# Half of one gated product per block handed from VectorE to ScalarE and GpSimd, in two of three blocks

## The chip, the cores and the metric

The kernel runs on one core of one Trainium2 chip. A core has five engines that work side by side, each through its own queue and in order: TensorE (matmuls, from SBUF into PSUM), VectorE, ScalarE, GpSimd, and SyncE, which here only issues DMAs. Engines wait for one another by semaphores. The metric is the device time of one execution in microseconds, the median of several runs. In the profile the engines are called PE, DVE, ACT, POOL and SP; PEld is TensorE's weight load.

## What is computed

An attention block with 32 inducing points over four batches of 12416 tokens, followed by a gated feed-forward layer of width 1536 over all 49664 tokens:

```python
def mab(q, kv):
    s = scale * (q @ kv.transpose(0, 2, 1))
    s = s - s.max(-1, keepdims=True)
    a = np.exp(s)
    a /= a.sum(-1, keepdims=True) + 1e-09
    return a @ kv
h = mab(I, x)                 # (B, 32, 128)
x = mab(x, h)                 # (B, 12416, 128), then seen as (49664, 128)

gate = 1.0 / (1.0 + np.exp(-(x @ w_gate)))
val = x @ w_val
return (gate * val) @ w_out
```

## The kernel before

The second attention's result is never formed. Its normalised weights `a2` (32 per token) are kept, and the products `h @ w_gate` and `h @ w_val` are folded into one small matrix `hw` per batch, so that gate and value of a token come from matmuls over 32 rows. The sigmoid is written as a tanh: gate times value is half of (tanh(g/2) + 1) times v, and the half is applied at the end.

*Blocks and steps.* 512 tokens (four chunks of 128) are a block; the 1536 features are twelve slices of 128, numbered j. A block is eight steps that alternate between two slices (wide, 1024 columns, two PSUM banks) and one slice (narrow, 512 columns, one bank): steps 0, 2, 4, 6 are wide, 1, 3, 5, 7 narrow. There are 96 such blocks, and four small ones of 128 tokens, one at the end of each batch: 776 steps in all, numbered t in the list `steps`.

*One step.* `gate(t)` (L545) issues the gate matmuls into `g_ps` (L535) and a tanh on ScalarE that writes `t` (L551). `product(t)` (L555) issues the value matmuls into `v_ps` (L535 too) and one VectorE instruction (L560) that adds 1 to `t`, multiplies by `v_ps` and writes `u`. PSUM has eight banks, all given out once: two for wide gates (`g2`), two for wide values (`v2`), one each for narrow gates (`g1`) and values (`v1`), one for side work (`m`), one for the accumulated result (`acc`). So a value matmul of a wide step waits until the product of the wide step before it has read `v_ps`, and a gate matmul until the tanh two steps earlier has read `g_ps`.

*The order.* It is written out by hand in the main loop (L690): for step t the product of t, then the gate of t+2, then in even steps a slot of side work (`beside`, L666), in odd steps projections (`project`, L580). `room` counts the projections that a call may issue, two units for each; before, it is 6 or 8, that is three or four. The queue of projections goes in order of j; each multiplies a slice of `u` by `wo16` into `acc` (L590). After a block's twelfth projection, ScalarE scales `acc` by one half into `o16` (L597, `o` in the profile), SyncE issues a DMA that transposes it into `on` (L599), and twelve steps later GpSimd issues the store to DRAM (L608). The next block's first projection waits until `o` has read `acc`.

*Side work.* `stage2` makes `a2` for the coming blocks: scores (L346), their maximum `nmx` on VectorE (L357), `hi` and `lo` on GpSimd (L361, L363), an Exp `e` on ScalarE (L379), the sums on GpSimd (L387), a reciprocal `rs` on VectorE (L405), `a2n` on GpSimd (L407), a transposing DMA into `a2r`. `stage1` does the first attention for the next batch: scores with their maximum `nm` (L169), an Exp `a1T` (L181), a transposing DMA, sums copied to `hst` by ScalarE (L217); `combine` joins the groups of a batch, with `hx` on GpSimd (L279, L290), and ends in `hw` (`hwt`, L336). Each is a generator that `beside` advances by one piece per slot; one holder at a time has the bank `m`. `stage2` is started 20 slots ahead of its use (`S2_LEAD`).

*Buffers.* `u` has six buffers of each width, `t` four.

Of the kernel before, what the change touches and what calls it, by code (L numbers as in the profile page):

```python
# [16 lines left out]
P = 128  # L17
# [3 lines left out]
S1_LAG = 6  # L21
S2_LEAD = 20


@with_exitstack
def kernel(
# [30 lines left out]
    s2p = ctx.enter_context(tc.tile_pool(name="s2p", bufs=2))  # L57
    up = ctx.enter_context(tc.tile_pool(name="up", bufs=6))
    tp = ctx.enter_context(tc.tile_pool(name="tp", bufs=4))
    op = ctx.enter_context(tc.tile_pool(name="op", bufs=8))  # L60


# [86 lines left out]

    summed = [0] * B  # L150

    def s1_dims(s):
# [3 lines left out]

    def s1_score(b, s, tag):
        c0, n = groups[s]
        ng, w, R = s1_dims(s)
        s1 = ps.tile([P, 512], F32, tag=tag, name="s1_ps")  # L160
        for g in range(ng):
            nc.tensor.matmul(  # L162
                s1[32 * g : 32 * g + 32, 0 : w * P],
                indT[:],
                xT[b][:, c0 + g * w : c0 + (g + 1) * w, :].rearrange("c j t -> c (j t)"),
                start=True,
                stop=True,
            )
        nc.vector.tensor_reduce(  # L169
            out=nm1s[b % 2][0:R, s : s + 1],  # L170
            in_=s1[0:R, 0 : w * P],
            axis=AX.X,
            op=ALU.max,
            negate=True,
        )
        return s1
# [12 lines left out]

    def s1_turn_pe(b, s, a1T):  # L190
        ng, w, R = s1_dims(s)
        aT = ps.tile([P, 4, P], F16, tag="m", name="aT_ps")
# [10 lines left out]

    def s1_sum(b, s, a1, tag):
        c0, n = groups[s]
        ng, w, R = s1_dims(s)
# [136 lines left out]

    def s2_score(b, c, j0, j1, s2):
        for j in range(j0, j1):
            nc.tensor.matmul(  # L346
# [20 lines left out]

    def s2_exp(n, s2, hi, lo):
        for t_, last in ((hi, False), (lo, True)):
            nc.tensor.matmul(  # L370
# [129 lines left out]
    for b in range(B):  # L500
        for s, (c0, n) in enumerate(groups):
            first_step[(b, s)] = len(steps)
            for k in range(0, n, BC):
# [5 lines left out]
                while j < NJ:  # L509
                    cnt = min(2 * per, NJ - j)  # L510
                    if nb == BC and idx % 2 == 1:
                        cnt = 1
                    steps.append(dict(b=b, c=c0 + k, nb=nb, j0=j, cnt=cnt))
                    j += cnt
# [40 lines left out]
    def product(t):  # L555
        st = steps[t]
        hidden_mm(st, "v")
        k, w = st["ext"]
        st["u"] = up.tile([P, k, 512], F16, tag=f"u{k}", name="u16")
        nc.vector.scalar_tensor_tensor(  # L560
            out=st["u"][:, :, 0:w],
            in0=st["t"][:, :, 0:w],
            scalar=1.0,
            in1=st["v"][:, :, 0:w],
            op0=ALU.add,
            op1=ALU.mult,
        )

    accs = {}
# [3 lines left out]
    for key in dict.fromkeys((st["b"], st["c"]) for st in steps):  # L573
        mine = [t for t in range(NST) if (steps[t]["b"], steps[t]["c"]) == key]
        of = {j: t for t in mine for j in range(steps[t]["j0"], steps[t]["j0"] + steps[t]["cnt"])}
        row = sorted(of)
        queue += [(of[j], j, j == row[0], j == row[-1]) for j in row]
    queue.reverse()

    def project(upto, now, room):  # L580
        while queue and queue[-1][0] < upto and room > 0:
# [4 lines left out]
            if first:  # L586
                accs[key] = ps.tile([P, 512], F32, tag="acc", name="acc_ps")
            acc = accs[key]
            k, col = place(st, j)
            nc.tensor.matmul(  # L590
                acc[:, 0:W], wo16[:, j, :], st["u"][:, k, col : col + W], start=first, stop=last
            )
            room -= 2 if st["nb"] == BC else 1
# [71 lines left out]

    def beside(slot):  # L666
        slot_now[0] = slot
# [6 lines left out]
        while work and work[0][0] <= slot:  # L674
            _, first, make = work.pop(0)
            active.append(dict(it=make(), ask=False, first=first))
        for gen in sorted(active, key=lambda e: e["first"]):
            advance(gen)
# [11 lines left out]
    for t in range(NST):  # L690
        product(t)
        gate(t + 2)
        if t % 2 == 0:
            beside(t // 2)
        else:
            project(t - 1, t, 6 if waiting(t - 1) <= 3 else 8)
        flush_stores(t)
# [32 lines left out]
```

## Time and profile before

| | us |
|---|---|
| median of three runs | 794.26 |
| lowest and highest | 793.11, 795.95 |
| the profiled execution | 795.01 |
| its span, first to last instruction | 793.1 |
| VectorE busy in the span | 745.4 |
| ScalarE busy | 672.8 |
| TensorE busy | 670.7 |
| GpSimd busy | 238.2 |
| products (L560), 388 wide and 388 narrow, mean | 1.219 and 0.676 |
| tanh (L551), 388 wide and 388 narrow, mean | 1.029 and 0.605 |
| `o` (L597), 96 of full width, mean | 0.605 |
| granted TensorE clock, mean | 0.967 |

A group of the profile shows a line, an engine and an operation, what it writes and reads, the count, then the busy time in us, the mean of one in ns, and the idle time of the engine just before these instructions with what ended it. The busy time of an engine is the union of its instructions' times; on VectorE and ScalarE an instruction's record reaches into the next one's by 0.1 us or so, so that starts lie closer together than durations say. In the timeline a line gives the start, the length, the engine and the group; neighbours of one kind are merged and counted (x3).

### The profile page before, as it was taken

What the parts mean: (1) busy time and instruction counts of PE and PEld (TensorE: products, weight loads), DVE (VectorE), ACT (ScalarE), POOL (GpSimd) and SP (SyncE); (2) the same over time, 40 slices, a digit from 0 to 9 for tenths busy, and PEclk for the clock granted to TensorE, in tenths of its full rate; (3) what the DMA queues carried; (4) which work ended last, traced back from release to release, by engine and by line L of the source; (5) the groups of instructions that cost most, each with busy time, mean ns of one, the idle gap of its engine ahead of it and who ended that gap; (6) DMA issues with size and microseconds to landing.
All of it is one profiled execution on the core that took longest, in us unless ns stands there. A gap on an engine that the chain in (4) does not pass through costs nothing.

```text
span 793.1 us, 13966 instructions
## 1 busy us (share of the span) xinstructions
PE 670.7 (85%) x4729; PEld 230.8 (29%) x4729; DVE 745.4 (94%) x948; ACT 672.8 (85%) x1001; POOL 238.2 (30%) x396
## 2 busy tenths in 40 slices
PE   6588889888888888888888888988888888888884
PEld 4222223222232222322222222322323222223221
DVE  4689999999999999999998999999999999999994
ACT  4389989888989999878988898988898898899993
POOL 4131341532331422444404123143233133133200
PEclk9679999999999999989999999999999999999997
DMA  9958654536439566355338754241431431441421
GB/s 178 204 108 168 120 111 84 103 77 116 87 75 198 95 102 138 81 98 100 64 80 163 131 93 91 57 81 47 83 86 43 90 87 28 100 87 40 103 60 46
DMA packets 171015, 77.44 MB, mean 98 GB/s; under 512 B 154784, under 2 KB 155328, under 8 KB 170944
## 3 DMA queue, kind: packets, MB, share of 16 engines
q1 hardware_dynamic: 150672, 37.23, 28.8%
q0 software_dynamic: 20272, 39.33, 21.0%
q8 instruction: 37, 0.61, 0.3%
q14 instruction: 34, 0.28, 0.1%
HBM read 27.80 MB, written 25.43 MB: 67 GB/s over the span
## 4 chain that ended last, share of the span: by engine, by line
DVE 42%; PE 24%; issue 21%; ACT 10%; DMA 2%; POOL 0%; POOLq 0%; ACTq 0%; DVEq 0%
DVE u L560 37%; PE acc_ps L590 11%; PE v_ps L535 9%; ACT t L551 8%; DMA xn<-in_x_dram 2%; DVE nmx L357 2%; PE s_ps L370 1%; DVE nm L169 1%; PE g_ps L535 1%; ACT a1T L181 1%; ACT o L597 1%; DVE rs L405 1%; DVE hwt L336 0%; PE hp_ps L210 0%; PE s_ps L346 0%
## 5 line engine op out<-in xcount | busy, mean ns | idle before, releaser
L560 DVE SCALAR_TENSOR_TENSOR u<-t,v_ps 128x1024 f16<-128x1024 f16 (+1 forms) x776 | 693.1, 947 | 19.0 <-PE g_ps L535 7.3
L551 ACT ACTIVATE t<-g_ps 128x1024 f16<-128x1024 f32 (+1 forms) x776 | 598.8, 817 | 81.5 <-PE g_ps L535 67.0
L535 PE MATMUL v_ps<-a2r,hwt 32*128 32x512 f16 (+1 forms) x1188 | 294.7, 374 | 94.8 <-DVE u L560 87.6
L590 PE MATMUL acc_ps<-u,wo 128*128 128x512 f16 (+1 forms) x1200 | 325.2, 383 | 1.4 <-ACT o L597 0.7
L535 PE MATMUL g_ps<-a2r,hwt 32*128 32x512 f16 (+1 forms) x1188 | 297.4, 381 | 0.8 <-ACT t L551 0.6
L535 PEld LDWEIGHTS <-hwt 32*128 32x128 f16 x2400 | 102.8, 91 | 355.0 <-issue 346.7
L590 PEld LDWEIGHTS <-wo 128*128 128x128 f16 x1200 | 86.1, 98 | 145.3 <-issue 99.3
L407 POOL TENSOR_TENSOR a2n<-e,rs 128x2048 f16<-128x2048 f16 (+2 forms) x28 | 87.3, 3119 | 82.2 <-DVE rs L405 73.7
L608 POOL DMA_DIRECT2D out_dram<-on x100 | 57.0, 570 | 143.8 <-DMA on<-o 134.1
L597 ACT ACTIVATE o<-acc_ps 128x512 f16<-128x512 f32 (+1 forms) x100 | 59.2, 592 | 9.5 <-PE acc_ps L590 7.1
L361 POOL CAST hi<-nmx 128x16 bf16<-128x16 f32 (+3 forms) x29 | 5.7, 195 | 203.1 <-DVE nmx L357 203.0
L387 POOL TENSOR_TENSOR sum<-e 128x256 f32<-128x256 f16 (+1 forms) x27 | 16.0, 591 | 70.2 <-ACT e L379 70.2
L387 POOL TENSOR_TENSOR sum<-sum 128x128 f32<-128x128 f32 (+3 forms) x108 | 31.3, 290 | 8.5
L76 POOL DMA_DIRECT2D xn<-in_x_dram x28 | 15.4, 557 | 11.1 <-DMA xn<-in_x_dram 7.2
L346 PE MATMUL s_ps<-hT,xT 128*128 128x32 f16 x388 | 18.2, 180 | 0.6
L181 ACT ACTIVATE a1T<-s_ps,nm 128x512 f16<-128x512 f32 (+1 forms) x28 | 17.9, 639 | 0.4 <-DVE nm L169 0.4
L169 DVE TENSOR_REDUCE nm<-s_ps 128x1 f32<-128x512 f32 (+1 forms) x28 | 17.3, 618 | 0.5 <-PE s_ps L162 0.5
L346 PEld LDWEIGHTS <-xT 128*128 128x128 f16 x388 | 13.5, 97 | 13.4 <-issue 13.1
L357 DVE TENSOR_REDUCE nmx<-s_ps 128x16 f32<-128x512 f32 (+3 forms) x29 | 17.3, 596 | 0.0
L379 ACT ACTIVATE e<-s_ps 128x512 f16<-128x512 f32 (+3 forms) x29 | 15.2, 524 | 1.5 <-PE s_ps L370 1.5
L454 ACT COPY xT<-xt_ps 128x1024 f16<-128x1024 f16 x6 | 6.1, 1012 | 10.8 <-DVE xT L453 10.8
L453 DVE COPY xT<-xt_ps 128x1024 f16<-128x1024 f16 x6 | 4.1, 692 | 9.6 <-PE xt_ps L451 9.6
(78 smaller groups left out, 182.1 us busy)
## 6 DMA issues: line engine op xcount, KB each, us to landing
out_dram<-on POOLq DMA_DIRECT2D x96, 256.0 KB, 2.6
xn<-in_x_dram POOLq DMA_DIRECT2D x24, 512.0 KB, 8.5
on<-o SPq DMA_TRANSPOSE x100, 2.4
a2r<-a2n SPq DMA_TRANSPOSE x28, 6.0
wg<-in_moe_w_gate_dram POOLq DMA_DIRECT2D x1, 384.0 KB, 16.4
wv<-in_moe_w_val_dram POOLq DMA_DIRECT2D x1, 384.0 KB, 16.5
wo<-in_moe_w_out_dram POOLq DMA_DIRECT2D x1, 384.0 KB, 16.2
xT<-xn SPq DMA_TRANSPOSE x21, 4.7
```

Source lines behind the costliest of these rows:

```text
L169: nc.vector.tensor_reduce(out=nm1s[b % 2][0:R, s : s + 1], in_=s1[0:R, 0 : w * P], axis=AX.X, op=ALU.max, negate=True,)
L181: nc.scalar.activation(out=a1T[0:R, 0 : w * P], in_=s1[0:R, 0 : w * P], func=AF.Exp, bias=nm1s[b % 2][0:R, s : s + 1], accum_out=l1s[b % 2 ...
L346: nc.tensor.matmul(s2[:, j, :], xT[b][:, c + j, :], hT16[b][:], start=(j == 0), stop=False, skip_group_check=True,)
L357: nc.vector.tensor_reduce(out=nmx[:, 0:n], in_=s2[:, 0:n, :], axis=AX.X, op=ALU.max, negate=True)
L387: nc.gpsimd.tensor_tensor(out=d[:, 0:n, :], in0=src[:, :, 0:w], in1=src[:, :, w : 2 * w], op=ALU.add)
L407: eng.tensor_tensor(out=a2n[:, 0:n, :, :], in0=e[:, 0:n, :].unsqueeze(2).to_broadcast((P, n, 4, m)), in1=rs[:, 0:n].unsqueeze(2).unsqueeze ...
L535: nc.tensor.matmul(pt[:, k, col : col + W], hw[st["b"]][r : r + 32, j // 2, :], a2r[r : r + 32, o : o + nb, :].rearrange("p j t -> p (j t) ...
L551: nc.scalar.activation(out=st["t"][:, :, 0:w], in_=st["g"][:, :, 0:w], func=AF.Tanh, scale=0.5)
L560: nc.vector.scalar_tensor_tensor(out=st["u"][:, :, 0:w], in0=st["t"][:, :, 0:w], scalar=1.0, in1=st["v"][:, :, 0:w], op0=ALU.add, op1=ALU. ...
L590: nc.tensor.matmul(acc[:, 0:W], wo16[:, j, :], st["u"][:, k, col : col + W], start=first, stop=last)
L597: nc.scalar.mul(out=o16[:, 0:W], in_=acc[:, 0:W], mul=0.5)
L608: nc.gpsimd.dma_start(ov[st["b"], :, c : c + nb, :], on[:, 0:nb, :])
```

## The change

`SHARE(block)` picks two of every three blocks, 64 in all. In these the wide product of step 0 is split: VectorE computes the first of its two slices (512 columns, `near`). For the second, ScalarE copies the value from PSUM to SBUF (`vc`, f32), GpSimd adds 1 to the second half of `t` (`t1`, f32) and multiplies the two (`far`, f16). The projection that reads `far` (j = 1) is put last in its block. `u` gets five buffers instead of six, `t` three instead of four.

The order changes in three places. The slot of side work two steps ahead of a split product is skipped (loads and new generators still enter, none is advanced). In other even steps where the side work has issued nothing that counts in `filled` (scores, transposes, sums and the correction matmuls of the Exp), one projection may be issued, if more than two are waiting and the next isn't the first of a block. In odd steps `room` is 2 (one projection) behind a split product, else 6 with up to four waiting (before: up to three) and 8 with more.

```diff
+def SHARE(block):
+    return block % 3 != 2
...
-    up = ctx.enter_context(tc.tile_pool(name="up", bufs=6))
-    tp = ctx.enter_context(tc.tile_pool(name="tp", bufs=4))
+    up = ctx.enter_context(tc.tile_pool(name="up", bufs=5))
+    tp = ctx.enter_context(tc.tile_pool(name="tp", bufs=3))
...
+    vp = ctx.enter_context(tc.tile_pool(name="vp", bufs=2))
...
-                    steps.append(dict(b=b, c=c0 + k, nb=nb, j0=j, cnt=cnt))
+                    steps.append(
+                        dict(b=b, c=c0 + k, nb=nb, j0=j, cnt=cnt, off=nb == BC and idx == 0 and SHARE(blocks))
+                    )
...
-        nc.vector.scalar_tensor_tensor(
-            out=st["u"][:, :, 0:w],
-            in0=st["t"][:, :, 0:w],
+        mine = 1 if st["off"] else k
+        near = nc.vector.scalar_tensor_tensor(
+            out=st["u"][:, 0:mine, 0:w],
+            in0=st["t"][:, 0:mine, 0:w],
             scalar=1.0,
-            in1=st["v"][:, :, 0:w],
+            in1=st["v"][:, 0:mine, 0:w],
             op0=ALU.add,
             op1=ALU.mult,
         )
+        if st["off"]:
+            vc = vp.tile([P, 512], F32, tag="vc")
+            far = nc.scalar.copy(out=vc[:], in_=st["v"][:, 1, :])
+            tc.declare_no_dep(far.ins, near.ins, reason="each reads a bank of its own")
+            t1 = vp.tile([P, 512], F32, tag="t1", bufs=1)
+            nc.gpsimd.tensor_scalar_add(out=t1[:], in0=st["t"][:, 1, :], scalar1=1.0)
+            st["far"] = vp.tile([P, 512], F16, tag="far", name="far", bufs=3)
+            nc.gpsimd.tensor_tensor(out=st["far"][:], in0=t1[:], in1=vc[:], op=ALU.mult)
...
-        row = sorted(of)
+        late = 1 if steps[mine[0]]["off"] else NJ
+        row = sorted(of, key=lambda j: (j == late, j))
...
-            nc.tensor.matmul(
-                acc[:, 0:W], wo16[:, j, :], st["u"][:, k, col : col + W], start=first, stop=last
-            )
+            u = st["far"][:] if st["off"] and k == 1 else st["u"][:, k, col : col + W]
+            nc.tensor.matmul(acc[:, 0:W], wo16[:, j, :], u, start=first, stop=last)
...
-    def beside(slot):
+    def beside(slot, rest):
...
+        if rest:
+            return
         for gen in sorted(active, key=lambda e: e["first"]):
             advance(gen)
...
         if t % 2 == 0:
-            beside(t // 2)
+            was = filled[0]
+            beside(t // 2, t + 2 < NST and steps[t + 2]["off"])
+            if filled[0] == was and waiting(t - 1) > 2 and not queue[-1][2]:
+                project(t - 1, t, 2)
         else:
-            project(t - 1, t, 6 if waiting(t - 1) <= 3 else 8)
+            room = 2 if steps[t - 1]["off"] else 6 if waiting(t - 1) <= 4 else 8
+            project(t - 1, t, room)
```

More of the change, by code (lines that the diff above doesn't have):

```diff
@@ L150 @@
     summed = [0] * B
+    filled = [0]
     def s1_dims(s):
@@ L157, in s1_score @@
     def s1_score(b, s, tag):
+        filled[0] += 1
         c0, n = groups[s]
@@ L190, in s1_turn_pe @@
     def s1_turn_pe(b, s, a1T):
+        filled[0] += 1
         ng, w, R = s1_dims(s)
@@ L204, in s1_sum @@
     def s1_sum(b, s, a1, tag):
+        filled[0] += 1
         c0, n = groups[s]
@@ L344, in s2_score @@
     def s2_score(b, c, j0, j1, s2):
+        filled[0] += 1
         for j in range(j0, j1):
@@ L368, in s2_exp @@
     def s2_exp(n, s2, hi, lo):
+        filled[0] += 1
         for t_, last in ((hi, False), (lo, True)):
```

## The prediction

> **What bounds the kernel now.** I read the page's busy shares first, then its slices, then the groups by shape, and last the timeline of a quiet stretch around 400 us. The page's part 1, and the rows of part 2 for the two engines that the change loads and unloads:
>
> ```profile
> PE 670.7 (85%) x4729; PEld 230.8 (29%) x4729; DVE 745.4 (94%) x948; ACT 672.8 (85%) x1001; POOL 238.2 (30%) x396
> ...
> DVE  4689999999999999999998999999999999999994
> ACT  4389989888989999878988898988898898899993
> ```
>
> VectorE is at nine tenths or more nearly everywhere between the start and the tail; ScalarE has about a tenth to give. The groups by shape (busy us, then mean ns of one):
>
> ```profile
> L560 DVE SCALAR_TENSOR_TENSOR u<-t,v_ps 128x1024 f16<-128x1024 f16 x388 | 472.8, 1219 | 16.9 <-PE g_ps L535 6.9 <-ACT t L551 4.4 <-ACT o L597 1.8
> ...
> L597 ACT ACTIVATE o<-acc_ps 128x512 f16<-128x512 f32 x96 | 58.1, 605 | 8.0 <-PE acc_ps L590 5.6
> ...
> L279 POOL TENSOR_TENSOR hx<-hst,w 128x896 f32<-128x896 f32 x3 | 5.0, 1677 | 23.4 <-ACT w L273 23.4
> ...
> L290 POOL TENSOR_TENSOR hx<-hx 128x384 f32<-128x384 f32 x3 | 3.0, 991 | 0.2
> ```
>
> The timeline of VectorE, ScalarE and TensorE (start us, length us) shows how tightly the steps are coupled:
>
> ```profile
> 399.87 1.22 DVE L560 SCALAR_TENSOR_TENSOR u<-t,v_ps 128x1024 f16<-128x1024 f16 x1
> 401.01 0.68 DVE L560 SCALAR_TENSOR_TENSOR u<-t,v_ps 128x512 f16<-128x512 f16 x1
> 401.64 1.22 DVE L560 SCALAR_TENSOR_TENSOR u<-t,v_ps 128x1024 f16<-128x1024 f16 x1
> ...
> 399.85 1.02 ACT L551 ACTIVATE t<-g_ps 128x1024 f16<-128x1024 f32 x1 [0.26 <-PE g_ps L535]
> 400.76 0.59 ACT L551 ACTIVATE t<-g_ps 128x512 f16<-128x512 f32 x1
> 401.24 0.60 ACT L597 ACTIVATE o<-acc_ps 128x512 f16<-128x512 f32 x1
> 401.72 1.05 ACT L551 ACTIVATE t<-g_ps 128x1024 f16<-128x1024 f32 x1
> ...
> 400.30 0.82 PE L590 MATMUL acc_ps<-u,wo 128*128 128x512 f16 x3
> ...
> 400.74 0.38 PE L590 MATMUL acc_ps<-u,wo 128*128 128x512 f16 x1
> 401.15 0.39 PE L535 MATMUL v_ps<-a2r,hwt 32*128 32x512 f16 x2
> 401.16 0.39 PE L535 MATMUL g_ps<-a2r,hwt 32*128 32x512 f16 x2
> 401.74 0.37 PE L535 MATMUL v_ps<-a2r,hwt 32*128 32x512 f16 x1 [0.20 <-DVE u L560]
> ```
>
> A wide product (401.64) follows the wide one before it (399.87) by 1.77 us. Its value matmul issues at 401.15, 0.06 after the wide product before it ended (399.87 + 1.22), because the wide value banks exist once; the product starts 0.49 after that. So the pair of steps is a loop, 1.22 + 0.06 + 0.49 = 1.77, and the narrow product only fills it. A block of eight steps (wide 0, 2, 4, 6; narrow 1, 3, 5, 7) is four loops, 7.09 us. ScalarE's own spacings, start to start: wide tanh to the next 0.91, narrow tanh 0.48, `o` 0.48. The wide tanh at 399.85 starts as the wide product ahead of its own does, so it ends some 0.75 before its product wants it. This lead is the cover on which the change draws.
>
> **The change, part by part.** The built order of the changed kernel has 64 copies, on ScalarE between the narrow tanh 1 and the wide tanh 2 of a block; they wait for TensorE alone. Time zero below is the start of the shortened product 0.
>
> *Removed.* The 1024-wide product becomes 512 wide, 1.22 to 0.68. Both banks must be read out before value matmul 2: VectorE ends at 0.68, and the copy, for which I take 0.60 from `o` (same shape in, other type out), starts with the value matmul's data at about -0.04 and ends at 0.56. The loop would be 0.68 + 0.06 + 0.49 = 1.23: 0.54 saved, 64 x 0.54 = 34.8 us. Bounds of the copy: the 128-wide `hst` copy took 0.28 (L217), the 1024-wide `xT` copy 1.01 (L454); with these the next term would be smaller or larger by nothing, since it is the start-to-start spacing that counts, 0.48 by `o`, and at most 0.9 by the 1024-wide tanh.
>
> *Added on ScalarE.* Tanh 2, which used to start at -0.03, now stands behind the copy: -0.04 + 0.48 = 0.44, end 1.46, and product 2 starts at 1.53 and not 1.23. That gives back 0.30 each, 64 x 0.30 = 19.2 us. It is nothing where other VectorE work fills the gap. Left of the saving: 0.24 a block.
>
> *What is late next.* Gate matmul 4 waits for the end of tanh 2 (1.46 + 0.05), its tanh starts 0.46 later at 1.97, tanh 5 at 2.88, and then comes the `o` of the block before, which the changed order puts after tanh 5 (before, after tanh 3): 3.36 to 3.97. The first projection of the block, at step 5, needs that `o` to free the single `acc` bank. TensorE is in order: it now has four projections there in 61 of 64 blocks (three before), one every 0.22 (400.30 to 400.74 is two). They start at 4.02, and TensorE is free for value matmul 6 at 4.89. Product 4 began at 1.53 + 1.77 = 3.30 and ended at 4.52, so matmul 6 could have gone at 4.58. Loss 0.31. A block without side work therefore takes 1.53 + 1.77 + 2.09 + 1.77 = 7.16 us against 7.09: +0.07, although VectorE has less to do.
>
> *With side work.* The order tells where it falls. In 34 of the 64 blocks a VectorE operation of about 0.5 (`nmx`, `nm`, `hwt`, mostly in step 2) stands between product 2 and product 6; it takes 0.51 in both kernels, ScalarE catches up under it, and the 0.31 vanishes. 20 of these have nothing more: 20 x -0.24 = -4.8. In 14 of them `e` or `a1T` also stands right behind tanh 2, which makes `o` 0.33 to 0.5 later; some 0.11 stays: 14 x -0.13 = -1.8. Of the blocks without such cover, 16 plain ones give 16 x 0.07 = +1.1, 9 with `e` or `a1T` there, at 0.07 and 0.33 to 0.5 more, 9 x 0.43 = +3.9, and in 4 the VectorE operation falls into step 0, under the 0.30 gap: 4 x -0.48 = -1.9. (One copy is in the first block and is counted with the plain ones.)
>
> *Side work skipped in the slot ahead.* It moves by two steps, much of it into step 0 of the same block, where TensorE's scores (0.36 for eight) and sums hide in the gap: 16 x -0.1 and 3 x -0.35 = -2.6, with 0 and -8 as bounds. About 12 side operations stand in front of the four projections: +1.8 (0 to 4). Lateness for its readers: the turned weights `a2r` are issued 13 to 21 steps before their use instead of 13 to 23, over 11 us, against 6.0 us median to land; `hwt` is made 39 steps ahead instead of 59. Nothing there reaches the path. SP's transposes keep their order apart from `on`, which goes two steps later.
>
> *Added on GpSimd.* The addition is 512 wide: at least 0.25 (the 16-wide L393), at most 0.90 (a quarter of the 3.61 of L407). The multiplication lies between the 384-wide 0.99 and the 896-wide 1.68: 1.16. Together 1.4 to 2.1 us, 64 times, some 90 to 130 us on an engine busy for 238. What waits: the last projection of the block, put last for it, eleven steps or some 10 us later; and tanh 6, which writes into the third wide `t` buffer and so waits for the addition. It starts at 3.8, so GpSimd may be 2 to 3 us late for nothing. Behind the multiplication in GpSimd's queue stand `hi`, `lo`, the sums, `a2n` and the output stores, each due two slots (3.5 us) later at the earliest. I price this at 0. Cover gone (an `a2n` of 3.6 right ahead of the addition), it would cost up to 1 us in some of the 23 places.
>
> The Trainium skill, GPSIMD Engine Reference, section "Engine selection", speaks against the edit: elementwise work with two inputs belongs on VectorE, GpSimd being about twice as slow. From its ratio I would estimate the multiplication at 1.35 instead of 1.16; the sum would not change, since this engine's time isn't on the path.
>
> *Rest.* The blocks left alone get a fourth projection in about half the cases, 0.02 each: +0.3. The last block's projections end two steps later: +0.5. Fewer buffers for `u` (5) still hold ten steps; no wait.
>
> Sum: -4.8 - 1.8 + 1.1 + 3.9 - 1.9 - 2.6 + 1.8 + 0.3 + 0.5 = -3.5 us. The profiled execution took 795.0 (span 793.1 and 1.9 around it), so 791.5; the median of the runs is 0.75 lower, so **791 us** after rounding.
>
> **Rivals.**
> *Only the copy is paid.* If the late `o` costs nothing (ScalarE recovers faster than I walk it, or side work covers nearly every block), the saving is 64 x 0.24 = 15.4, with the two step-0 terms (1.9 and 2.6) 19.9: 795.0 - 19.9 = 775 us. For it: part 2's ScalarE row leaves a tenth idle. Against it: 3.97 against 3.72, where the first projection could start, is read from tight rows.
> *ScalarE and the projections decide.* Each block loses 0.30 at the copy; if `o` is on average late enough to cost 0.35 more (plain 0.31, 0.64 with an `e` ahead) whatever VectorE's side work covers, the losses are 64 x 0.65 = 41.6 against 34.8: +7, so 802 us; at 0.8 each, 811. It decides from 0.54 a block on. For it: three engines are coupled through single PSUM buffers, and the granted clock of TensorE, 0.967 on average, stretches projections in places. Against it: the 34 blocks with cover.
> *The copy waits for the shortened product* (the two not being independent after all): copy from 0.68, product 2 at 2.25 and thus 0.48 later than before, 64 x 0.48 = 31, so 825 us. The wait list of the built order names TensorE alone; hardly likely.
>
> **How the numbers follow.** The forecast as told, 783 to 797: 0.40. Only the copy paid: 0.25. ScalarE and the projections: 0.33. The copy waits: 0.02. I call 0.3% (2.4 us) what a measurement can tell. Of the forecast, 0.24 lies below 791.9, 0.12 within, 0.04 above; the first rival is faster throughout; of the second 0.03 is within and 0.30 slower. So faster 0.49, same 0.15, slower 0.36. The range runs from 771 (the first rival with more of its side work hidden) to 811 (the second at 0.8), and leaves out the third and the outer parts of the others, less than 2 in 10.
>
> **What will show it.** Product 2 starting about 1.5 after product 0 in a copied block, with VectorE's idle time before it put down to tanh; idle time before product 6, put down to a value matmul that came behind four projections and `o`; VectorE busy about 711 and ScalarE about 704; GpSimd near 350. No tanh should wait for GpSimd. I am wrong if product 2 starts at 1.25 or at 1.8 and more, if the wait before product 6 is absent or above 0.6, or if GpSimd ends the longest waits.

## The result, and the profile after

| | us |
|---|---|
| kernel before, in the same comparison | 794.75 (793.11 to 795.95) |
| changed kernel, median of four runs | 836.12 (824.78 to 842.05) |
| ratio (see below), with its 95% interval | 1.0414 [1.0346, 1.0483] |

The change makes the kernel 4% slower; the forecast was 791, in a range from 771 to 811. The ratio is that of the two runs with the higher mean granted clock, 824.78 us at 0.966 and 830.33 at 0.955; the other two, 841.9 and the profiled 842.05 (span 840.0), ran at 0.936. So pairs of steps (from one wide product's start to the next one's) are compared below at full clock, and the stretches at half clock are an item of their own.

The page of the changed kernel, the parts that answer to those shown of before (busy us and share; then tenths by slice, PEclk being the granted clock):

```profile
PE 716.0 (85%) x4729; PEld 233.1 (28%) x4729; DVE 722.1 (86%) x948; ACT 699.6 (83%) x1065; POOL 415.3 (49%) x524
...
DVE  4589999989877998995898899999998998989993
...
PEclk9689999999988999996799999999999999999995
```

VectorE did get less work, 722 us against 745, and its share fell from 94% to 86%: no engine is now busy nine tenths throughout. What ended the idle time is in the groups by shape (busy us, mean ns of one, idle time just before and its releasers):

```profile
L575 DVE SCALAR_TENSOR_TENSOR u<-t,v_ps 128x1024 f16<-128x1024 f16 x324 | 395.0, 1219 | 70.3 <-PE g_ps L549 47.8 <-ACT t L565 9.4 <-PE v_ps L549 2.4
...
L588 POOL TENSOR_SCALAR t<-t 128x512 f32<-128x512 f16 x64 | 95.3, 1489 | 168.2 <-ACT t L565 167.8
...
L590 POOL TENSOR_TENSOR far<-t,vc 128x512 f16<-128x512 f32 x64 | 81.0, 1266 | 8.7 <-ACT vc L585 3.7
...
L585 ACT COPY vc<-v_ps 128x512 f32<-128x512 f32 x64 | 37.5, 586 | 18.8 <-PE g_ps L549 18.2
```

The wide products wait 70.3 us (16.9 before), mostly for TensorE. TensorE itself waits for two things that hardly held it before, as the lists of waits have it (total us, times, longest; first two lines before, then changed):

```profile
PE g_ps L535 <- ACT t L551: 1.3, 2, 0.7
...
PE acc_ps L590 <- ACT o L597: 0.7, 1, 0.7
...
PE g_ps L549 <- ACT t L565: 18.9, 55, 0.7
PE acc_ps L615 <- ACT o L620: 18.3, 19, 1.7
```

The split itself does what it was meant to. In the timeline of the changed kernel around a split product (start us, length us):

```profile
412.69 0.59 ACT L585 COPY vc<-v_ps 128x512 f32<-128x512 f32 x1 [0.57 <-PE g_ps L549]
413.18 1.03 ACT L565 ACTIVATE t<-g_ps 128x1024 f16<-128x1024 f32 x1
...
412.76 0.69 DVE L575 SCALAR_TENSOR_TENSOR u<-t,v_ps 128x512 f16<-128x512 f16 x1 [0.46 <-PE g_ps L549]
413.62 1.87 DVE L575 SCALAR_TENSOR_TENSOR u<-t,v_ps 128x512 f16<-128x512 f16 x2 [0.17 <-PE g_ps L549]
```

The shortened product starts at 412.76, the copy 0.07 ahead of it, the tanh 0.49 after the copy; the entry at 413.62 is the narrow product and the next wide one, which starts at 414.27. That is 1.51 after the shortened one, where the loop of before takes 1.77.

What costs the time is elsewhere. This is the chain of waits of the changed kernel between 765 and 769 us, a block that is not split (start us, length us, what):

```profile
764.85 0.43 PE acc_ps L615 x2
...
765.74 0.02 ACT t L565
...
766.66 0.60 ACT o L620
...
767.30 0.81 PE acc_ps L615 x3
768.11 0.32 PE v_ps L549 x2
...
768.54 0.16 DVE u L575
```

And the queues of TensorE and VectorE in the same place:

```profile
765.76 1.82 DVE L575 SCALAR_TENSOR_TENSOR u<-t,v_ps 128x1024 f16<-128x1024 f16 x2
768.54 1.22 DVE L575 SCALAR_TENSOR_TENSOR u<-t,v_ps 128x1024 f16<-128x1024 f16 x1 [0.96 <-PE g_ps L549]
...
765.59 0.39 PE L615 MATMUL acc_ps<-far,wo 128*128 128x512 f16 x1
...
767.30 0.81 PE L615 MATMUL acc_ps<-u,wo 128*128 128x512 f16 x3 [0.99 <-ACT o L620]
768.04 0.39 PE L549 MATMUL v_ps<-a2r,hwt 32*128 32x512 f16 x2
```

The last projection of the block before (765.59) was issued in an even step, the first three of the new block in the odd step right after. The first needs `o`, and `o` stands on ScalarE behind the wide tanh of 765.74. TensorE waits 0.99 us at the head of its queue, then issues three projections, and only then the value matmul (768.04) that VectorE lacks. From wide product (765.76, merged with the narrow one) to wide product (768.54) this pair takes 2.77 us, not 1.77. Of the 19 waits of TensorE for `o`, 18 are in pairs of this kind, all in blocks that are not split.

Sorting all 380 pairs by what the order issues in them gives the balance. The base is 1.77, plus what VectorE's own side work takes; the excess is summed, in us, for the profiles of both kernels and of a later run, the changed order without the split:

| pairs | before | changed | order alone |
|---|---|---|---|
| split product in front | | -17.0 | |
| same place, not split | | | +4.0 |
| last projection in the even step, first three in the odd one | | +17.3 | +17.2 |
| four projections that begin a block | -0.1 | +12.0 | +9.7 |
| two or three projections that end a block, mostly behind the split | +1.1 | +13.4 | +1.7 |
| other pairs at full clock | +8.8 | +5.1 | +2.8 |
| pairs slowed by half clock | +8.0 | +31.5 | +18.9 |
| sum | +17.8 | +62.3 | +54.3 |

The difference of 44.5 between the first two sums is that of the spans (46.9) but for the ends. Per block: 7.83 us where split (7.62 before), 8.55 where not (7.60 before). The +4.0 of the order alone is nearly all one pair of 5.68 us at 371.7, in which VectorE's copy `lb`, 0.23 us where GpSimd is idle, takes 3.52 and ends at 376.88, as GpSimd's `a2n` does (376.80).

### The profile page after: what moved, and what is told of

Same layout as the page of the kernel before. It is cut to its first block, busy times and chain, and to the rows that moved or that the text cites. A ratio compares the mean times of both kernels' runs of the same rounds, so it can differ in the third digit from the quotient of the medians.

```text
span 840.0 us, 14231 instructions
## 1 busy us (share of the span) xinstructions
PE 716.0 (85%) x4729; PEld 233.1 (28%) x4729; DVE 722.1 (86%) x948; ACT 699.6 (83%) x1065; POOL 415.3 (49%) x524
## 4 chain that ended last, share of the span: by engine, by line
PE 41%; DVE 25%; issue 16%; ACT 14%; DMA 2%; POOL 2%; ACTq 0%; POOLq 0%; DVEq 0%
PE acc_ps L615 22%; DVE u L575 20%; PE v_ps L549 13%; ACT t L565 8%; ACT o L620 3%; PE g_ps L549 3%; DMA xn<-in_x_dram 2%; DVE nmx L368 1%; ACT a1T L189 1%; DVE nm L177 1%; PE s_ps L382 1%; ACT e L391 1%; PE s_ps L357 1%; POOL a2n L419 0%; POOL xn L82 0%
## 5 line engine op out<-in xcount | busy, mean ns | idle before, releaser
L575 DVE SCALAR_TENSOR_TENSOR u<-t,v_ps 128x512 f16<-128x512 f16 (+1 forms) x776 | 670.2, 904 | 89.3 <-PE g_ps L549 60.6
L615 PE MATMUL acc_ps<-u,wo 128*128 128x512 f16 (+1 forms) x1136 | 344.5, 399 | 21.7 <-ACT o L620 18.3
L549 PE MATMUL v_ps<-a2r,hwt 32*128 32x512 f16 (+1 forms) x1188 | 300.7, 388 | 52.3 <-DVE u L575 50.6
L549 PE MATMUL g_ps<-a2r,hwt 32*128 32x512 f16 (+1 forms) x1188 | 302.0, 389 | 20.0 <-ACT t L565 18.2
L549 PEld LDWEIGHTS <-hwt 32*128 32x128 f16 x2400 | 94.0, 92 | 333.5 <-issue 314.5
L588 POOL TENSOR_SCALAR t<-t 128x512 f32<-128x512 f16 x64 | 95.3, 1489 | 168.2 <-ACT t L565 167.8
L615 PEld LDWEIGHTS <-wo 128*128 128x128 f16 x1200 | 98.0, 100 | 206.2 <-issue 166.5
L590 POOL TENSOR_TENSOR far<-t,vc 128x512 f16<-128x512 f32 x64 | 81.0, 1266 | 8.7 <-ACT vc L585 3.7
L585 ACT COPY vc<-v_ps 128x512 f32<-128x512 f32 x64 | 37.5, 586 | 18.8 <-PE g_ps L549 18.2
L615 PE MATMUL acc_ps<-far,wo 128*128 128x512 f16 x64 | 25.6, 400 | 0.0
```

What stands on the lines that cost most here:

```text
L549: nc.tensor.matmul(pt[:, k, col : col + W], hw[st["b"]][r : r + 32, j // 2, :], a2r[r : r + 32, o : o + nb, :].rearrange("p j t -> p (j t) ...
L575: near = nc.vector.scalar_tensor_tensor(out=st["u"][:, 0:mine, 0:w], in0=st["t"][:, 0:mine, 0:w], scalar=1.0, in1=st["v"][:, 0:mine, 0:w], ...
L585: far = nc.scalar.copy(out=vc[:], in_=st["v"][:, 1, :])
L588: nc.gpsimd.tensor_scalar_add(out=t1[:], in0=st["t"][:, 1, :], scalar1=1.0)
L590: nc.gpsimd.tensor_tensor(out=st["far"][:], in0=t1[:], in1=vc[:], op=ALU.mult)
L615: nc.tensor.matmul(acc[:, 0:W], wo16[:, j, :], u, start=first, stop=last)
```

## The experiments

"Clock" below is the range of the mean granted clock over a kernel's runs; the kernel before had 0.957 to 0.977 in all comparisons.

**One part alone or taken back.** First the split, its buffers and its late projection with the order of before:

```diff
-            beside(t // 2, t + 2 < NST and steps[t + 2]["off"])
-            if filled[0] == was and waiting(t - 1) > 2 and not queue[-1][2]:
-                project(t - 1, t, 2)
+            beside(t // 2, False)
...
-            room = 2 if steps[t - 1]["off"] else 6 if waiting(t - 1) <= 4 else 8
-            project(t - 1, t, room)
+            project(t - 1, t, 6 if waiting(t - 1) <= 3 else 8)
```

> The split, its buffers and the late place of the GpSimd projection stay; the order rules of before return (no projection in even steps, three or four in odd ones, no slot skipped). Theory A (the new order costs most, the split itself gives 0.30 per split block and pays part of it back through `o`): 785 to 805. Rival B (the split itself is what costs, through the copy and GpSimd): 815 or more. Rival C (GpSimd's or ScalarE's work lowers the granted clock): a mean clock below 0.95.

Measured: 806.81 us, ratio 1.0157 [1.0118, 1.0196], clock 0.963 to 0.972. Even in the order of before, the kernel with the split is 12 us slower. The shortened pair gains nothing there: with three projections behind it, it takes 1.69, with four 1.90 (medians of 26 each), on average what it took unsplit. The loss lies in other pairs of the profile: the first pairs of the blocks that are not split, now mostly with four projections, take 1.90 for 1.77 (some 4 us), and the pairs of step 4 in split blocks and those slowed by half clock lose some 3 us more each.

Then no block split, so that the new rules of the order hardly act and the fewer buffers remain:

```diff
-    return block % 3 != 2
+    return False
```

> No block is split; the buffers (five `u`, three `t`) and the new rules of the order stay, which without a split differ in few places from those of before (no slot is skipped, nine pairs have another number of projections). Theory A: the buffers cost nothing, 793 to 797. Rival (fewer buffers make waits of their own): above 800.

Measured: 795.26, 1.0004 [0.9982, 1.0027]. The buffers cost nothing.

Then the changed kernel with one more condition in the even step, so that a block's last projection is not issued there:

```diff
-            if filled[0] == was and waiting(t - 1) > 2 and not queue[-1][2]:
+            if filled[0] == was and waiting(t - 1) > 2 and not queue[-1][2] and not queue[-1][3]:
```

> Edit to the changed kernel: the single projection of an even step may not be the last of its block. In the changed kernel's trace 17 pairs of steps have the last projection in the even step and three projections of the next block, the first waiting for `o`, in the odd step; such a pair takes 2.77 us instead of 1.77 at full clock. Theory A (the late `o` stands at the head of TensorE's queue there): 17 x 1.0 less, so 808 to 815 against 825 for the changed kernel's undisturbed runs, and no pair of 2.77 is left. Rival B (the granted clock or GpSimd makes the loss): within 5 us of 825.

Measured: 822.25, 1.0345 [1.0307, 1.0382], clock 0.934 to 0.940. The pairs of 2.77 are gone and blocks that are not split fall from 8.55 to 8.05, but the run missed its range, for the clock fell too. Near the clock of the profiled run of the changed kernel (842 at 0.936) it is 17 to 20 us faster (825.28 at 0.934, 821.83 and 822.68 at 0.938), which is that item of the balance.

And no skipped slot:

```diff
-            beside(t // 2, t + 2 < NST and steps[t + 2]["off"])
+            beside(t // 2, False)
```

> The changed kernel without the skipped slot of side work. Theory A (the skip matters little, since it only moves side work by two steps): within 6 us of the changed kernel's 825. Rival (the skip delays or bunches side work and costs): 805 to 815. The other rival (it protects the copy): above 835.

Measured: 824.76, 1.0378 [1.0344, 1.0412], clock 0.960 to 0.964, the clock at which the changed kernel took 824.78 (0.966). The skipped slot is no large term.

**The fours, the clock, GpSimd, another order.** At most three projections in the call that begins a block, with the condition above:

```diff
-            room = 2 if steps[t - 1]["off"] else 6 if waiting(t - 1) <= 4 else 8
+            room = 2 if steps[t - 1]["off"] else 6 if waiting(t - 1) <= 4 or queue[-1][2] else 8
```

> The kernel of e1_guard, with at most three projections in the call that begins a block (four before; the fourth goes elsewhere). In the trace of e1_guard 82 undisturbed pairs with four of these take 1.93 us against 1.77. Theory A (the fourth projection and the late `o` cost 0.16 a pair, together): 808 to 816 against 822. Rival B (any fourth projection costs the same wherever it stands, since TensorE needs 0.31 us from a projection to the next value matmul): 816 to 824, and pairs with four elsewhere take about 1.89.

Measured: 823.01, 1.0367 [1.0327, 1.0407], clock 0.937 to 0.948. The fours moved into the middle of the blocks (some 50 pairs, +18 us there); the projections have to go somewhere.

The value matmuls of the pair behind the split issued twice, to keep TensorE busier, with the condition:

```diff
+        if what == "v" and st.get("again"):
+            for j in range(st["j0"], st["j0"] + st["cnt"]):
...
```

> The kernel of e1_guard, in which the value matmuls of the step pair behind a split product are issued twice, to the same result (128 more matmuls, where TensorE waits for tanh anyway). e1_guard ran at a granted clock of 0.934 to 0.940 in all its runs and the changed kernel at 0.936 to 0.966; in the traces most of the half-clock stretches follow 3.4 us in which TensorE's records cover only 0.5 to 0.67. Theory A (the clock is halved after stretches in which TensorE has little to do): clock 0.95 or more and 805 to 818. Rival B (it is halved for load, or the clock has nothing to do with these gaps): clock 0.94 or less and 822 or more.

Measured: 825.29, 1.0396 [1.0351, 1.0441], clock 0.937 to 0.945: hardly an effect on the clock.

GpSimd's two instructions left out; the projection of that slice reads ScalarE's copy of the value:

```diff
-            vc = vp.tile([P, 512], F32, tag="vc")
+            vc = vp.tile([P, 512], F16, tag="far", name="far", bufs=3)
...
-            nc.gpsimd.tensor_scalar_add(out=t1[:], in0=st["t"][:, 1, :], scalar1=1.0)
...
-            nc.gpsimd.tensor_tensor(out=st["far"][:], in0=t1[:], in1=vc[:], op=ALU.mult)
+            st["far"] = vc
```

> The changed kernel without GpSimd's two operations: the copy writes f16 and the projection reads it, so the addition of 1 and the product with tanh are left out for that slice. Theory A (GpSimd is off the path, although its two operations took 2.76 us and not the 1.4 to 2.1 forecast): within 6 us of the changed kernel's 825 to 836. Rival B (GpSimd's work delays `hi`, `lo`, sums or tanh): 10 us or more below it.

Measured: 834.64, 1.0511 [1.0469, 1.0553], clock 0.938 to 0.948. The changed kernel took 842.05 at 0.936 and 830.33 at 0.955, so at like clocks little, some 2 us, is gained without GpSimd's 2.75 us per split block: they are off the path, as forecast.

An order in which a block's last projections go to step 5, its first to step 7, one behind the split:

```diff
+            if i == 5 and not queue[-1][2]:
+                n = min(left, 5)
+            elif split:
+                n = {1: 1, 3: 2 if left <= 7 else 3}.get(i, 3)
+            else:
+                n = 3
...
+            project(t - 1, t, 2 * n)
```

> The split with another order of projections: a block's first three at its step 7, at most one behind the split product, none between copy and the next gate, the last always in step 5, so that `o` comes two pairs ahead of the copy; a fourth (seldom a fifth) only with the last. Theory A (the split gives 0.30 a split block, each fourth projection costs 0.12, a fifth 0.45, and nothing else is lost): 64 x 0.30 - 50 x 0.12 - 12 x 0.45 = 8 us faster than before, 782 to 792. Rival B (the split costs in ways that the order doesn't reach, the granted clock above all): 800 or more.

Measured: 818.52 (814.58 to 835.91), 1.03 [1.0255, 1.0345], clock 0.921 to 0.958. A miss: blocks left alone are back to 7.65, but split blocks take 7.90; the pair behind the split takes 1.85 without side work, 2.33 to 2.52 with it (1.77 without, in the kernel before).

**TensorE behind the split.** The repeat of above as one matmul of the full 128 rows into the value bank, with the condition:

```diff
+        if what == "v" and st.get("again"):
+            nc.tensor.matmul(
+                pt[:, 0, :], wo16[:, 0, :], wg16[:, 0:2, :, :].rearrange("p i t f -> p (i t f)"), start=True, stop=True
+            )
```

> The kernel of e1_guard with one more matmul of the full array (128 rows, 512 columns) ahead of the value matmuls of the pair behind each split product, into a bank that the value matmul then overwrites, so the output stays. It fills some 0.2 of the 0.5 us in which TensorE stands there for tanh. e6_fill, with repeated matmuls of 32 rows, left the clock at 0.937 to 0.945. Theory A (the clock follows how much of the array works, and the repeats of 32 rows were too light): clock 0.955 or more, 805 to 815. Rival B (these gaps don't decide the clock): 0.945 or less, 820 or more.

Measured: 817.54, 1.0289 [1.0252, 1.0326], clock 0.949 to 0.957 (0.934 to 0.940 without the matmul): the clock rose where the 32-row repeat had left it.

The other order with up to two projections between the value and the gate matmuls of the pair behind the split:

```diff
+        if spot(t) == (2, True):
...
+            project(t - 1, t, 2 * fit)
```

> The order of e9_sched, with two projections put between the value and the gate matmuls of the pair behind a split product, where TensorE stood for tanh, and so one or two fewer behind them; hardly a call of four is left. e9_sched took 818.5 at clocks of 0.944 to 0.958, and its split blocks 7.90 us against 7.62 before. Theory A (what takes the saving is TensorE: it stands in order at the gate matmul behind the copy, and has no room to catch up with its projections): split blocks at 7.5 or less, 782 to 797. Rival B (the copy itself, tanh or the clock takes it): split blocks still at 7.75 or more, 808 or more.

Measured: 807.6 (803.89 to 811.36), 1.0166 [1.0127, 1.0205], clock 0.945 to 0.959. Split blocks 7.69, others 7.615. One pair of 9.16 us remains, seen on GpSimd and TensorE in this run's timeline:

```profile
365.82 3.61 POOL L419 TENSOR_TENSOR a2n<-e,rs 128x2048 f16<-128x2048 f16 x1
369.38 1.68 POOL L289 TENSOR_TENSOR hx<-hst,w 128x896 f32<-128x896 f32 x1
371.14 2.32 POOL L300 TENSOR_TENSOR hx<-hx 128x384 f32<-128x384 f32 x3
...
374.63 0.21 POOL L372 CAST hi<-nmx 128x1 bf16<-128x1 f32 x1
...
374.89 0.19 PE L382 MATMUL s_ps<-hi,identb 128*128 128x32 bf16 x1 [6.22 <-POOL hi L372]
```

TensorE holds its whole queue for a correction matmul whose input, 0.2 us of work, stands behind 7.6 us on GpSimd. The changed kernel has the same stall at 3.05 us.

This without copy and multiplication, the projection reading tanh + 1 (the product with the value is left out for that slice):

```diff
-            far = nc.scalar.copy(out=vc[:], in_=st["v"][:, 1, :])
...
-            nc.gpsimd.tensor_tensor(out=st["far"][:], in0=t1[:], in1=vc[:], op=ALU.mult)
+            nc.gpsimd.tensor_scalar_add(out=st["far"][:], in0=st["t"][:, 1, :], scalar1=1.0)
```

> The kernel of e11_ahead without ScalarE's copy and GpSimd's multiplication: the projection of the far slice reads tanh + 1, so the product with the value is left out for that slice. Theory A (0.24 of the 0.54 us saved on VectorE goes to tanh standing behind the copy, as measured by pairs of 1.47 us where the value banks alone would allow 1.23): undisturbed split pairs at 1.25 or less, and 10 to 18 us less than e11_ahead's 807.6. Rival B (the pair is held by TensorE's order as much as by ScalarE): pairs at 1.4 or more, within 6 us of 807.

Measured: 807.28, 1.015 [1.0114, 1.0185], clock 0.934 to 0.949. About half of the split pairs fell from 1.47 to between 1.24 and 1.30, so the copy's price was real; the median time did not follow, the clock being lower. At like clocks it did in part: 804.35 and 804.37 at 0.949, beside 811.36 at 0.947 and 809.54 at 0.951 with the copy.

The run before last with `hi` and `lo` of the small blocks on VectorE, against the long stall:

```diff
-        nc.gpsimd.tensor_copy(out=hi[:, 0:n], in_=nmx[:, 0:n])
+        eng = nc.vector if n == 1 else nc.gpsimd
+        eng.tensor_copy(out=hi[:, 0:n], in_=nmx[:, 0:n])
```

> The kernel of e11_ahead with `hi` and `lo` of the four small blocks (128x1) on VectorE and not on GpSimd. In e11_ahead TensorE stands once for 6.2 us at the correction matmul of a small block, which waits for `hi` while GpSimd works off the two split operations, `a2n` and `hx`. Theory A (GpSimd's added work reaches the path there, and only there): 5 to 8 us less than 807.6, about 801, with no pair above 4.5 us. Rival B (the wait moves to the next thing that GpSimd owes, `hx`): within 3 us.

Measured: 816.58 (811.41 to 826.88), 1.0275 [1.0241, 1.0308], clock 0.927 to 0.950: slower. The stall went to other places, one of them like this in the timelines of VectorE and GpSimd:

```profile
176.08 1.22 DVE L375 TENSOR_TENSOR lo<-nmx,hi 128x1 bf16<-128x1 f32 x1
...
177.60 2.58 DVE L308 COPY lb<-lsum 128x128 f32<-128x128 f32 x1
...
176.02 1.26 POOL L591 TENSOR_TENSOR far<-t,vc 128x512 f16<-128x512 f32 x1
...
178.39 1.70 POOL L289 TENSOR_TENSOR hx<-hst,w 128x896 f32<-128x896 f32 x1
```

An operation on one column, 0.19 us on GpSimd, takes 1.22 on VectorE and ends as GpSimd's multiplication does (177.30 and 177.28). Two more of the four take 2.71 and 2.15 and end with GpSimd's `a2n` (374.50 and 374.49) and `hx` (564.98 and 564.95); the fourth takes 0.16. The copy `lb` takes 2.58 and ends at 180.18, just after `hx` (180.09). It takes 0.23 where GpSimd is idle (at 31.55 in the kernel before); the other three there take 0.89 and also end with an `hx`.

**The order alone.** The changed order to the letter, projections and skipped slots included, with no product split: no copy, no GpSimd.

```diff
-                        dict(b=b, c=c0 + k, nb=nb, j0=j, cnt=cnt, off=nb == BC and idx == 0 and SHARE(blocks))
+                        dict(b=b, c=c0 + k, nb=nb, j0=j, cnt=cnt, off=False, as_if=nb == BC and idx == 0 and SHARE(blocks))
...
-            room = 2 if steps[t - 1]["off"] else 6 if waiting(t - 1) <= 4 else 8
+            room = 2 if steps[t - 1]["as_if"] else 6 if waiting(t - 1) <= 4 else 8
```

> The changed kernel's order to the letter (skipped slots, room of one projection behind step 0 of the same 64 blocks, j = 1 last, projections in even steps, the buffers), but no product is split: VectorE does all of it, and there is no copy and nothing more for GpSimd. Theory A (the order is what costs: 17 pairs of a last and three first projections at 1.0, some 65 calls of four at 0.16, and a lower granted clock): 815 to 835, clock 0.94 to 0.96, and pairs of 2.7 or more where the last and the first projections meet. Rival B (the order is harmless by itself and costs only together with the copy): 800 or less at the clock of before (0.965 or more).

Measured: 834.76 (832.91 to 836.69), 1.0519 [1.049, 1.0549], clock 0.945 to 0.954. The order alone makes the whole loss, with the same main items in the balance above. In the one pair of runs at like clocks (0.954 and 0.955) the split on top of it gains 2.6 us (832.91 against 830.33).

**What sets the clock.** Of the 38 us in the profile of the order alone (833.47 against 795.01), 27 are the two patterns of projections and 11 half clock (18.9 against 8.0). Half clock comes in stretches of 3.4 us, or multiples; the table of the order-alone run by such stretches shows one (busy us of each engine with counts, then PEclk):

```profile
core 0: us, PE busy (x) PEld busy (x) DVE busy (x) ACT busy (x) POOL busy (x), PEclk, DMA share, GB/s
...
758.10:761.50 3.40, 2.68 (x18) 0.86 (x16) 3.31 (x5) 3.02 (x4) 1.84 (x1) 1.00 0.21 43
761.50:764.90 3.40, 2.42 (x20) 0.92 (x17) 3.40 (x6) 2.88 (x4) 2.33 (x2) 1.00 0.19 55
764.90:768.30 3.40, 3.32 (x14) 0.69 (x13) 2.40 (x3) 2.13 (x4) 0.96 (x3) 0.50 1.32 266
```

From 761.5 VectorE has no gap and TensorE is busy 2.42 of 3.40 us, but only three of its matmuls are projections; the next stretch runs at half clock, and VectorE loses 1.0 us. In all 19 traces (two kernels, seventeen experiments) I laid a grid of 3.413 us on the half-clock stretches and weighted each matmul's streaming time at full clock (0.216 us for 512 columns, the spacing of projections in the traces) by the share of the array's 128 rows that it uses (gate and value matmuls, with 32 rows, count a quarter). Full-clock stretches from some 75 us on, by that share of the time, and how many were followed by half clock:

```
below 0.36     111 of 111
0.36 to 0.40    35 of 103
above 0.40       8 of 3603
```

The best single bound on this share sorts 24 of the stretches wrongly; on busy time without the weights it sorts more than 100 wrongly. Long idle time is not what they have in common: only 7 of the 154 stretches followed by half clock have a gap of more than 3 us on TensorE. Of these traces 15 were there when the rule was formed; the test came after, and the four later traces have 14 of 14, 6 of 14 and none of 777. The order alone got its odd calls of fewer than three projections filled up to three by full-height matmuls over a tile of zeros, 210 in all, which add nothing to the result; in the best order with the split (side work advanced in every slot) the same was done in step 5, in all blocks, in none, and in the blocks that are not split.

```diff
+    zero = vp.tile([P, 512], F16, tag="zero", name="zero", bufs=1)
+    nc.gpsimd.memset(zero[:], 0.0)
...
+            while fill > 0 and not first:
+                nc.tensor.matmul(acc[:, 0:W], wo16[:, j, :], zero[:, 0:W], start=False, stop=False)
+                fill -= 1
```

> The order of the changed kernel without its split (as in the run of the order alone, 834.8 us), with every odd call that issues fewer than three projections filled up to three by matmuls of full height over a tile of zeros into the open accumulator (210 in all, mostly behind the place of the split product, where TensorE waits 0.46 and 0.20 us for VectorE, so that they should cost nothing there). Theory H: TensorE's clock is halved after a stretch of 3.4 us in which its matmuls, weighted by the share of the array's rows that they use (32-row matmuls a quarter), cover less than some 0.38 of the time; in the traces so far 82 of 83 stretches below 0.36 were followed by half clock and 8 of some 2,800 above 0.40. The fill lifts most thin stretches of this order above 0.40: single half-clock stretches in the middle fall from 12 to at most 5, the mean clock from 0.95 to 0.96 or more, the time to 818-829. Theory R (the thin places have nothing to do with the clock, and work added to an engine that works in order only delays it): clock 0.945-0.955, 834-845.

Measured: 827.61 (825.99 to 828.28), 1.0415 [1.0394, 1.0436], clock 0.962 to 0.967. A kernel with 210 matmuls more, none of them useful, is 7 us faster, the intervals being apart; half clock set in 4 times after the first 75 us, 12 times without them. One such place, behind the position of the split, in its timeline:

```profile
690.89 0.60 PE L619 MATMUL acc_ps<-zero,wo 128*128 128x512 f16 x2
691.34 0.38 PE L621 MATMUL acc_ps<-u,wo 128*128 128x512 f16 x1
```

The pairs that wait for `o` (16 at full clock, median 2.77) and the fours (1.93) are still there: what is left over the kernel before is mostly the order's pattern.

> The best order with the split so far (two projections ahead of the pair behind the split, 807.6), its side work advanced in every slot, and the call at step 5 filled up to three with zero matmuls (88 in all). Theory H: against the next run, the same without the fill, the clock rises by 0.005 to 0.015 and the time falls by 3 to 8; 788-799 in all. Theory R: no difference in clock, and up to 5 us slower than the next run.

Measured: 803.92 (798.43 to 806.43), 1.0105 [1.0069, 1.0142], clock 0.956 to 0.970.

> The best order with the split so far, its side work advanced in every slot instead of skipping the one ahead of a split product. If the stall of 9.2 us (a correction matmul that waits for GpSimd) comes from the skipped slots, it is gone, as in the changed kernel with the skip taken back, where no pair was longer than 4 us: 797-803. If it comes from GpSimd's new work alone, it stays: 805-810.

Measured: 803.06 (802.77 to 803.3), 1.0108 [1.0087, 1.0128], clock 0.952 to 0.953; no pair above 4 us, so the long stall came from the skipped slots together with GpSimd's queue (with skipped slots, but without GpSimd's two instructions, that wait was 0.3 us at most).

> The previous kernel with the zero fill (803.9 us) with the fill kept to the blocks that are not split, 51 matmuls in all. In the run before, the fill raised the clock from 0.953 to 0.96, but the split blocks rose from 7.65 to 7.73 us, 61 x 0.075 = 4.6, since TensorE has no slack behind the split. Theory H: unsplit blocks stay near 7.63, split blocks return to 7.65 or so, and the single long half-clock stretch of the kernel without fill (23.9 us, blocks of 12.05 and 11.44 instead of 7.6, some 8 us lost) does not come back: 794-800, so about level with the kernel before, clock 0.958-0.97. Rival: the split blocks are what thins TensorE's work, and without a fill there the clock falls back to 0.953: 801-805.

Measured: 803.06 (798.71 to 806.04), 1.0102 [1.0073, 1.0132], clock 0.949 to 0.964. Of these three the fill in all blocks raised the clock (0.956 to 0.970, without it 0.952 to 0.953), as the rule has it, but the time stayed: filling all blocks costs 0.075 in each split one (7.73 against 7.65), and filling the others alone leaves long half-clock stretches near 160 and 430 us in the profile. Split blocks stay at 7.65 in the best case, 7.62 before. No version with the split beat the kernel before.

## Why the prediction was wrong

*The step that failed* is the one on the blocks left alone: "the blocks left alone get a fourth projection in about half the cases, 0.02 each: +0.3". They lose 0.95 each (8.55 against 7.60), 32 x 0.95 = 30 us in the profiled execution: some 17 in the pairs that wait for `o`, some 13 in pairs slowed by half clock. The order without the split shows the same kind of loss (8.22). I had walked the new order for a split block and taken the rest as the old loop with one matmul more. The order's even-step rule excludes a block's first projection but not its last; when the last goes there, the next odd call begins the new block at once, and `o` stands behind a wide tanh. Removing that one case took the 17 us out.

*The mis-sized term.* "One every 0.22" holds between projections. From the last projection to the next value matmul the start-to-start spacing is 0.31 to 0.32 (in the split timeline 413.45 to 413.77, beside 0.22 between projections, 415.67 to 415.89). Four projections that begin a block are thus late by 0.16 (1.93 for 1.77), with the split or without it: +12 us. (The few calls of four in the kernel before take 1.77 to 1.89, so the count alone does not set it.) In split blocks I had 0.31 for them and for `o` together, which was too much: TensorE never waits for `o` there, and the loss is 0.16. I had nothing for the pair behind the split, which pays 13.4: there TensorE stands at the gate matmul that waits for the tanh behind the copy, and the two or three projections after it come late.

*What the sum did not hold* is the clock. I took the mean of 0.967 as given and used it only in a rival. The changed order thins TensorE's full-height work behind the split product, and half clock then costs 31.5 us against 8.0 in the two profiles. But the profiled run has the lowest clock of the four; at the clock of before (0.966) the changed kernel still takes 824.78, so most of the loss is not the clock's.

*What was right.* The pair in front: forecast 1.53, measured 1.47 (median of 47), so a gain of 0.30 and not 0.24, 17 us in the balance. Copy 0.586 (0.60 taken), with its price confirmed by the run without it (about 0.2). One tanh only is put down to GpSimd in the waits, 1.0 us behind `lo`, and its time is off the path (415 us busy, forecast 350: the addition takes 1.49 where I had at most 0.90, the multiplication 1.27, between the 1.16 and the 1.35 of the two estimates; 64 x 2.755 = 176). VectorE 722 (711), ScalarE 700 (704).

*Rivals.* "ScalarE and the projections decide", 802 to 811, was the nearest: it has the right engines and the wrong blocks, and no clock. The split alone on the old order would not have reached 791 either: it took 806.81.

*Open.* The bound of the clock's rule within 0.36 to 0.40, and whether some order lets the split pay: at a clock like before's, 0.964, the best run was 798.71, against about 795 of the kernel before at 0.965.

## What to carry to other kernels

A rule that changes an order acts in every place where its condition holds: list the distinct patterns that it makes (here, by what is issued in each pair of steps) and price each one, above all where a group's last and the next one's first now stand side by side. An engine that takes its queue in order gains nothing from a shortened instruction elsewhere if its own queue is what comes next. Work taken out of a stretch of TensorE's queue can slow its clock in the next one, so look at the thinnest 3.4 us, not at the mean.

## What the runs showed of the hardware

*The clock follows weighted work, not idleness.* In these 19 traces half clock came after stretches with little weighted work (table above), mostly without long idle time. Within one kernel the time moves with the mean clock by 4 to 6 us for 0.01 (after: 842.05 at 0.936, 824.78 at 0.966; order alone: 836.69 at 0.945, 832.91 at 0.954). The Trainium skill, TensorE: Matmul & The Clock Gate, section "Part 1: The HAM clock gate", says that the clock has two states and falls to half after an idle window of some 3.4 us on a free-running grid; the two states (1.00 and 0.50) and the 3.4 us agree with the traces, the idle window doesn't: 2.42 of 3.40 us busy was followed by half clock, and work of 32 rows did not count for what its time is (the repeat of such matmuls left the clock at 0.937 to 0.945, full-height ones raised it).

*VectorE held by GpSimd.* The two lines of 1.22 and 2.58 us above fit what the Trainium skill, SBUF — State Buffer, section "SBUF: two separate sides", states: the two engines share a pair of ports that one instruction holds to its end. VectorE's copy of 0.23 us took up to 3.52 while GpSimd worked; the wide product, which reads one operand from PSUM, keeps its 1.219 in both kernels.

*On GpSimd an addition with one input takes longer than a multiplication with two:* 1.489 us (128x512, f16 in, f32 out) against 1.266 (f32 in, f16 out).
